# Reciprocals spread through DRAM, value tiles composed on GpSimd, convolution weights transposed first

## The chip, the cores and the metric

One core of one Trainium2 chip. The metric is the device time of one execution, in microseconds (us), less is better. Engine names in the profile: PE is TensorE, PEld its weight loads, DVE is VectorE, ACT is ScalarE, POOL is GpSimd, SP is SyncE.

## The reference

Blockwise causal attention, followed by a gated linear unit whose gate is a causal convolution of five taps. Cut to what matters:

```python
# q, k, v: (8 batches, 8 heads, 576, 64); mask in blocks of 64
scores = where(block_i >= block_j, (q @ k.T) / 8, -1e9)
attn = exp(scores - max) / (sum(...) + 1e-9)
x = (attn @ v)                      # heads side by side: (8, 576, 512)
gate = sigmoid(causal_conv5(x, conv_w))
out = (gate * (x @ w_val)) @ w_out
```

## The kernel before

The kernel works in turns `t`, four per batch, each of a pair of heads. Scores of turn `t`, values of turn `t - 6` and the gated unit of turn `t - 9` are interleaved. Once per batch the softmax denominators are made with matmuls against a one-hot matrix; VectorE takes their reciprocals, which must then reach all 128 partitions. These are the parts that matter here (`vec` keeps VectorE's program order; `load` issues from GpSimd, queue 0; outputs go from SyncE, queue 1):

```python
    def compose_v(b):            # value tiles padded and regrouped
        t = vts[b]
        d = v16p.tile([128, 4, 4, 64], fp16, tag="vd")
        s4 = t[:, :, :].rearrange("p (n t) d -> p n t d", n=4)
        vec.tensor_copy(out=d[0:64, :, :, :], in_=s4[0:64, :, 5:9, :])
        for i in range(4):
            vec.tensor_copy(out=d[64:128, :, i, :], in_=s4[64:128, :, 4, :])
        z = vzs[b % 2]
        vec.tensor_copy(out=z[0:64, :, 0:5, :], in_=s4[0:64, :, 0:5, :])
        vec.tensor_copy(out=z[64:128, :, 5, :], in_=s4[64:128, :, 4, :])
    ...
    def den(b):
        dn = psG.tile([128, 9, 32], fp32, tag="G")       # one of 4 PSUM buffers
        ...                                              # 88 matmuls
        ri = rp.tile([128, 288], fp32, tag="ri")
        vec.reciprocal(out=ri[:, :], in_=dn[:, :, :].rearrange("p j x -> p (j x)"))

    def spread(b):
        ri = ris.pop(b)
        for h in range(2):
            for u in range(2):
                for e in range(2):
                    r0, r1 = 32 * (2 * h + u), 32 * (2 * h + e)
                    move = vec if b == 0 and h == 0 else nc.gpsimd
                    move.tensor_copy(out=rqs[b % 2][r0:r0 + 32, e, :], in_=ri[r1:r1 + 32, :])

    def pv(t):
        ...
        rb = rp.tile([128, 2, 9, 32], fp32, tag="rb")
        vec.stream_shuffle(out=rb..., in_=rqs[b % 2]..., mask=[n] * 32)
        for part, (lo, hi) in enumerate(((0, 5), (5, 9))):
            x = psG.tile([128, nb, 64], fp32, tag="G")
            ...                                          # value matmuls into x
            vec.tensor_tensor(out=xb[...], in0=x[...], in1=rb[...], op=ALU.mult)
    ...
    for t in range(NT + LAG):
        b, r = divmod(t, 4)
        scores(t, 0)
        if t % 2 == 0: load_pair(t // 2 + 3)             # one q and one k load
        if r == 0: load_v(b)
        if t in (2, 3, 6, 7): weights(t // 4, t % 2 * 2)
        if r == 0 and b >= 1: compose_v(b - 1)
        if t <= 4: conv_weights(t - 1)                   # -1: transpose, 0 to 3: diagonals
        ...
        if r == 0 and b >= 1: den(b - 1)
        ...
        pv(t - 6)
        ...
        if r == 1 and b >= 1: spread(b - 1)
        gate(...); val(...); project(...)
```

The softmax here doesn't subtract the row's maximum and nothing guards it: scores larger than these inputs give would overflow.

## Time and profile before

| | before |
|---|---|
| median of the first three runs | 242.03 us (241.86 to 243.42) |
| span of the profiled run | 242.0 us |
| PE busy | 220.4 us, 91% |
| DVE busy | 159.6 us, 66% |
| POOL busy | 65.8 us, 27% |

The head of the page. The rows of digits cut the span into 40 slices of 6 us; a digit is the busy share in tenths (9 is 90% or more), and PEclk is TensorE's granted clock.

```profile
span 242.0 us, 7696 instructions
PE 220.4 (91%) x3352; PEld 146.6 (61%) x3352; DVE 159.6 (66%) x340; ACT 139.1 (57%) x232; POOL 65.8 (27%) x110
PE   0799978799989998999989998999989997999993
PEclk9997788979999999999999999999999999999999
DMA  5999999969707990399108980192002200321205
```

TensorE binds from the ninth slice (about 51 us) on. Before that there is a ramp, in which the DMA engines are full and the clock is granted at half speed part of the time. The table of stretches shows the same: each line is a stretch in us, then busy time and count per engine, the granted clock, the DMA share (over 1 where packets overlap) and GB/s.

```profile
core 0: us, PE busy (x) PEld busy (x) DVE busy (x) ACT busy (x) POOL busy (x), PEclk, DMA share, GB/s
7.00:51.00 44.00, 37.45 (x654) 26.36 (x655) 34.28 (x63) 29.19 (x40) 20.74 (x30) 0.85 1.36 157
71.00:90.00 19.00, 19.00 (x256) 11.89 (x254) 12.05 (x25) 12.75 (x23) 6.29 (x9) 1.00 1.05 150
90.00:97.00 7.00, 6.23 (x156) 4.57 (x154) 6.64 (x15) 3.40 (x7) 1.21 (x3) 1.00 0.01 2
```

From 71 to 90 us TensorE has no gap at all. The stretch from 90 to 97 holds a denominator turn, and there 0.77 us are idle. The list of waits (who waited for whom: us in total, times, longest) says for what:

```profile
PE cv L43 <- DVE ri L56: 5.1, 6, 1.2
```

The timeline of VectorE around one such turn (start us, duration us, engine, line, operation, output and inputs, count) shows why, and the last line is TensorE's:

```profile
65.29 1.07 DVE L56 COPY d<-t 64x1024 f16<-64x1024 f16 x5
66.37 0.72 DVE L56 COPY vz_72<-t 64x1280 f16<-64x1280 f16 x2
67.12 1.96 DVE L56 RECIPROCAL ri<-dn 128x288 f32<-128x288 f32 x1
...
69.13 0.77 PE L43 MATMUL cv<-xb_67,diag 128*128 128x288 f16 x5 [0.77 <-DVE ri L56]
```

The convolution's second half needs the PSUM buffer that the reciprocal reads (PSUM tiles are what this kernel's matmuls write into). Composing (`d`, `vz`) delays the reciprocal a little: the denominator matmuls had ended at 66.8.

The first batch in the ramp, its reciprocals and their first use:

```profile
28.52 1.96 DVE L56 RECIPROCAL ri<-dn 128x288 f32<-128x288 f32 x1 [1.20 <-PE dn L43]
...
36.50 0.80 DVE L56 STREAM_SHUFFLE rb<-rq_70 128x576 f32<-128x576 f32 x1
37.40 0.82 DVE L56 TENSOR_TENSOR xb_67<-x,rb 128x320 f16<-128x320 f32 x2
```

There are 7 us between the end of the reciprocals and their first use.

### The profile page before, as it was taken

How to read it: one execution, taken by the hardware profiler on the slowest of the kernel's cores; microseconds unless marked ns; L12 is line 12 of the kernel's file. 1: busy time of each engine (PE TensorE's matmuls, PEld its weight loads, DVE VectorE, ACT ScalarE, POOL GpSimd, SP SyncE). 2: the span in 40 equal slices, each digit the busy share in tenths (PEclk: the TensorE clock that was granted, in tenths of full speed). 3: DMA queues.
4: the chain of work that ended last, by engine and by line, in shares of the span. 5: the costliest groups of instructions: out<-in, count | busy, mean ns of one | idle time of the engine just before them, and what ended most of it. 6: DMA issues, size and time to landing. Idle time of an engine off the chain costs nothing.

```text
span 242.0 us, 7696 instructions
## 1 busy us (share of the span) xinstructions
PE 220.4 (91%) x3352; PEld 146.6 (61%) x3352; DVE 159.6 (66%) x340; ACT 139.1 (57%) x232; POOL 65.8 (27%) x110
## 2 busy tenths in 40 slices
PE   0799978799989998999989998999989997999993
PEld 0565755566765576556756566556755674676661
DVE  3377798967895489846695489756694368556330
ACT  2549686466837664665827755665737853333442
POOL 8950093390058001820057002410050005000000
PEclk9997788979999999999999999999999999999999
DMA  5999999969707990399108980192002200321205
GB/s 95 177 187 195 186 89 192 141 89 163 50 3 126 208 137 3 33 242 197 47 0 147 210 114 5 45 153 88 36 3 89 87 3 3 143 76 63 113 3 213
DMA packets 52010, 25.13 MB, mean 104 GB/s; under 512 B 38149, under 2 KB 47365, under 8 KB 51978
## 3 DMA queue, kind: packets, MB, share of 16 engines
q0 software_dynamic: 46784, 15.21, 58.5%
q1 hardware_dynamic: 5184, 9.44, 10.6%
q8 instruction: 26, 0.43, 0.7%
q14 instruction: 6, 0.05, 0.1%
q10 hardware_dynamic: 10, 0.01, 0.0%
HBM read 30.42 MB, written 9.44 MB: 165 GB/s over the span
## 4 chain that ended last, share of the span: by engine, by line
PE 76%; DVE 12%; ACT 3%; issue 3%; DMA 3%; POOL 0%; ACTq 0%; DVEq 0%; POOLq 0%
PE cv L43 16%; PE ps L43 15%; PE ot L43 13%; PE vp L43 12%; PE tr L131 10%; PE x L43 9%; DVE ri L56 5%; DVE d L56 2%; DMA t<-in_k_dram 2%; ACT pt L168 2%; DVE gv L56 2%; DVE qkT L56 2%; PE dn L43 2%; ACT pt L194 1%; DVE vz_73 L56 1%
## 5 line engine op out<-in xcount | busy, mean ns | idle before, releaser
L168 ACT ACTIVATE pt<-ps 128x1024 f16<-128x1024 f32 (+1 forms) x96 | 75.6, 825 | 16.2 <-PE ps L43 15.6
L56 DVE COPY qkT<-tr 128x768 f16<-128x768 f16 (+1 forms) x62 | 49.6, 836 | 33.4 <-PE tr L131 32.3
L43 PE MATMUL ps<-qkT 64*64 64x64 f16 (+10 forms) x608 | 45.6, 257 | 3.8 <-ACT pt L194 1.4
L328 ACT ACTIVATE th<-cv 128x288 f32<-128x288 f32 x64 | 26.2, 412 | 32.9 <-PE cv L43 30.9
L356 ACT ACTIVATE ob<-ot 128x512 f32<-128x512 f32 x36 | 21.7, 602 | 33.8 <-PE ot L43 28.7
L56 DVE SCALAR_TENSOR_TENSOR gv<-th,vp 128x288 f16<-128x288 f32 x64 | 26.9, 446 | 18.4 <-PE vp L43 18.0
L43 PEld LDWEIGHTS <-qkT 64*64 64x64 f16 (+1 forms) x608 | 21.3, 105 | 28.1 <-issue 19.8
L43 PEld LDWEIGHTS <-diag 128*128 128x128 f16 x320 | 28.9, 98 | 14.8 <-issue 6.2
L43 PE MATMUL ot<-w_out_sb,gv 128*128 128x512 f16 x144 | 35.8, 380 | 0.0
L131 PE MATMUL tr<-ident_59,t 128*64 128x128 f16 x576 | 28.5, 242 | 6.8 <-DMA t<-in_q_dram 5.5
L259 POOL COPY rq_71<-ri 32x288 f32<-32x288 f32 x32 | 13.4, 420 | 65.1 <-DVE ri L56 63.5
L259 POOL COPY rq_70<-ri 32x288 f32<-32x288 f32 x28 | 11.8, 420 | 65.5 <-DVE ri L56 64.1
L43 PE MATMUL x<-pt,t 128*64 128x256 f16 (+3 forms) x384 | 28.0, 257 | 1.7 <-issue 1.7
L131 PEld LDWEIGHTS <-t 128*64 128x64 f16 x576 | 20.0, 121 | 13.9 <-DMA t<-in_q_dram 5.5
L43 PEld LDWEIGHTS <-w_val_sb 128*128 128x128 f16 x256 | 23.1, 98 | 7.6 <-issue 0.2
L194 ACT ACTIVATE pt<-ps 128x512 f16<-128x512 f32 x32 | 19.1, 598 | 10.5 <-PE ps L43 9.1
L43 PEld LDWEIGHTS <-t 128*64 128x64 f16 x384 | 18.5, 113 | 10.5 <-issue 8.1
L43 PEld LDWEIGHTS <-gv 128*128 128x128 f16 x144 | 12.7, 98 | 13.7 <-issue 2.1
L43 PE MATMUL cv<-xb_67,diag 128*128 128x288 f16 x120 | 17.6, 292 | 1.5 <-DVE ri L56 1.5
L43 PE MATMUL cv<-xb_68,diag 128*128 128x288 f16 x120 | 17.1, 286 | 1.5 <-DVE ri L56 1.5
L56 DVE RECIPROCAL ri<-dn 128x288 f32<-128x288 f32 x8 | 15.7, 1958 | 1.4 <-PE dn L43 1.2
L46 POOL DMA_DIRECT2D t<-in_v_dram x8 | 14.6, 1826 | 5.1 <-PE x L43 4.7
(51 smaller groups left out, 234.7 us busy)
## 6 DMA issues: line engine op xcount, KB each, us to landing
out_dram<-ob SPq DMA_DIRECT2D x36, 256.0 KB, 2.1
t<-in_q_dram POOLq DMA_DIRECT2D x16, 288.0 KB, 7.0
t<-in_k_dram POOLq DMA_DIRECT2D x16, 288.0 KB, 7.9
t<-in_v_dram POOLq DMA_DIRECT2D x8, 576.0 KB, 13.1
w_val_sb<-in_moe_w_val_dram POOLq DMA_DIRECT2D x2, 256.0 KB, 13.6
w_out_sb<-in_moe_w_out_dram POOLq DMA_DIRECT2D x2, 256.0 KB, 6.7
conv_nat<-in_moe_conv_w_dram ACTq DMA_DIRECT2D x1, 10.0 KB
```

Of the source, the lines that this page charges most:

```text
L43: tc.keep_in_program_order(nc.tensor.matmul(**kw))
L46: tc.keep_in_program_order(nc.gpsimd.dma_start(**kw))
L56: return lambda **kw: tc.keep_in_program_order(f(**kw))
L131: tc.keep_in_program_order(nc.tensor.transpose(out=tr[64 * z:64 * z + 64, s, :], in_=q16[hb, w][:, z, c, :], identity=ident16[:, :]))
L168: nc.scalar.activation(out=pt[:, o:o + w], in_=src, func=AF.Exp, bias=0.0, scale=0.125)
L194: nc.scalar.activation(out=pt[:, 2048:2560].rearrange("p (h x) -> p h x", h=2), in_=ps[:, :, 0:256], func=AF.Exp, bias=0.0, scale=0.125)
L259: move.tensor_copy(out=rqs[b % 2][r0:r0 + 32, e, :], in_=ri[r1:r1 + 32, :])
L328: nc.scalar.activation(out=th[:, HF * hf:HF * hf + HF], in_=cv[:, :], func=AF.Tanh, bias=0.0, scale=0.5)
L356: nc.scalar.mul(out=ob[:, :], in_=ot[:, :], mul=0.5)
```

## The change

Its intent is to unload VectorE. The reciprocals are written once to DRAM and read back by four broadcast reads per batch, so that the 32 shuffles and 64 copies of the on-chip way go. Composing of the value tiles moves to GpSimd, one turn earlier. The transpose of the convolution weights moves ahead of the first q and k transposes.

```diff
+    rscr = nc.dram_tensor("r_scratch", [B, 128, 288], fp32, kind="Internal")
@@ compose_v
-        vec.tensor_copy(out=d[0:64, :, :, :], in_=s4[0:64, :, 5:9, :])
-        for i in range(4):
-            vec.tensor_copy(out=d[64:128, :, i, :], in_=s4[64:128, :, 4, :])
+        nc.gpsimd.tensor_copy(out=d[0:64, :, :, :], in_=s4[0:64, :, 5:9, :])
+        nc.gpsimd.tensor_copy(out=d[64:128, :, :, :],
+                              in_=s4[64:128, :, 4:5, :].to_broadcast([64, 4, 4, 64]))
         ... the two copies into z likewise
@@ spread: the copies go
+        nc.sync.dma_start(out=rscr[b], in_=ris.pop(b)[:, :])
+        rb = rp.tile([128, 4, 2, 9, 32], fp32, tag="rb", name="rb")
         for h in range(2):
+            for e in range(2):
+                r0 = 32 * (2 * h + e)
+                nc.sync.dma_start(
+                    out=rb[64 * h:64 * h + 64, :, e, :, :].rearrange("p n j y -> p n (j y)"),
+                    in_=rscr[b, r0:r0 + 4, :].rearrange("(a r) x -> a r x", a=1).to_broadcast(
+                        [64, 4, 288]))
+        rbs[b] = rb
@@ pv: the stream_shuffle goes
-                in1=rb[:, :, lo:hi, :].rearrange("p e j y -> p j e y"),
+                in1=rbs[b][:, n, :, lo:hi, :].rearrange("p e j y -> p j e y"),
@@ setup and loop
+    conv_weights(-1)
     for part in range(3):
         trans(0, part)
-        if r == 0 and 1 <= b <= B:
-            compose_v(b - 1)
-        if t <= 4:
+        if r == 3 and b < B:
+            compose_v(b)
+        if 1 <= t <= 4:
             conv_weights(t - 1)
         if r == 0 and 1 <= b <= B:
             den(b - 1)
+            spread(b - 1)
-        if r == 1 and 1 <= b <= B:
-            spread(b - 1)
```

More of the change, by code (lines that the diff above doesn't have):

```diff
@@ L75 @@
            for i in range(NXB)]
-    rqs = [cpool.tile([128, 2, 288], fp32, tag=f"rq{i}", name=f"rq{i}") for i in range(2)]
     vzs = [cpool.tile([128, 4, 6, 64], fp16, tag=f"vz{i}", name=f"vz{i}") for i in range(2)]
@@ L110, in compose_v @@
         s4 = t[:, :, :].rearrange("p (n t) d -> p n t d", n=4)
-        vec.tensor_copy(out=d[0:64, :, :, :], in_=s4[0:64, :, 5:9, :])
-        for i in range(4):
-            vec.tensor_copy(out=d[64:128, :, i, :], in_=s4[64:128, :, 4, :])
+        nc.gpsimd.tensor_copy(out=d[0:64, :, :, :], in_=s4[0:64, :, 5:9, :])
+        nc.gpsimd.tensor_copy(out=d[64:128, :, :, :],
+                              in_=s4[64:128, :, 4:5, :].to_broadcast([64, 4, 4, 64]))
         z = vzs[b % 2]
-        vec.tensor_copy(out=z[0:64, :, 0:5, :], in_=s4[0:64, :, 0:5, :])
-        vec.tensor_copy(out=z[64:128, :, 5, :], in_=s4[64:128, :, 4, :])
+        nc.gpsimd.tensor_copy(out=z[0:64, :, 0:5, :], in_=s4[0:64, :, 0:5, :])
+        nc.gpsimd.tensor_copy(out=z[64:128, :, 5, :], in_=s4[64:128, :, 4, :])
         vts[b] = (t, d, z)
@@ L248, in den @@
         ris[b] = ri
+    rbs = {}
     def spread(b):
-        ri = ris.pop(b)
+        nc.sync.dma_start(out=rscr[b], in_=ris.pop(b)[:, :])
+        rb = rp.tile([128, 4, 2, 9, 32], fp32, tag="rb", name="rb")
         for h in range(2):
-            for u in range(2):
-                for e in range(2):
-                    r0, r1 = 32 * (2 * h + u), 32 * (2 * h + e)
-                    move = vec if b == 0 and h == 0 else nc.gpsimd
-                    move.tensor_copy(out=rqs[b % 2][r0:r0 + 32, e, :], in_=ri[r1:r1 + 32, :])
+            for e in range(2):
[5 more added lines that the diff above has]
+        rbs[b] = rb
     def pv(t):
@@ L266, in pv @@
         xb = xbs[b % NXB]
-        rb = rp.tile([128, 2, 9, 32], fp32, tag="rb")
-        vec.stream_shuffle(out=rb[:, :, :, :].rearrange("p e j y -> p (e j y)"),
-                                 in_=rqs[b % 2][:, :, :].rearrange("p e x -> p (e x)"),
-                                 mask=[n] * 32)
         for part, (lo, hi) in enumerate(((0, 5), (5, 9))):
```

## The prediction

> **What bounds the kernel now.** The page gives TensorE (PE) 220.4 us busy of 242.0 (91%), VectorE (DVE) 66%, GpSimd (POOL) 27%. By stretches, PE is busy without a gap from 71 to 90, 97 to 117, 124 to 144, 151 to 171 and 203 to 235 us: PE binds from about 51 us on. Its 21.6 us of idle time are about 5.5 at the start, 4 after the last matmul, 5 to 6 in the ramp from 7 to 51 us (DMA row at 9, granted clock down to 0.8), and a gap of 0.77 us in each later denominator turn (list of waits: "PE cv <- DVE ri 5.1 us, 6 times"). So 40 us less DVE work cannot become 40 us less time.
>
> **What the change does.** From DVE it removes 32 shuffles (25.5 us), the composing of value tiles (14 us, 1.8 per batch) and four copies (1.4). From POOL it removes 60 copies of 420 ns (25 us) and adds 32, about 4 us per batch (estimate from those 420 ns for 288 elements). It adds one 147 KB write and four 295 KB broadcast reads per batch on the SyncE queue: 8192 pieces of 1152 B in all. The output's 2048-byte pieces took 88 ns; I estimate 55 to 60 ns for these, 4 us of all 16 engines per batch. It moves 1.9 us of small fp32 matmuls (at 10.4 us) into the wait for the first q load, which ends at 5.4.
>
> **What of it is critical.**
> - Later turns: in the timeline the denominator matmuls end at 66.8 and the reciprocal runs 67.1 to 69.1, only 0.3 us late for DVE's composing. The next convolution group still waits for its PSUM buffer: gap 0.77 becomes about 0.4, a gain of 2 to 2.5 us in all.
> - Weights first: gain 1 to 1.5 us. DVE relief in the ramp: 0.5 to 1.
> - First batch: reciprocal at 28.5 to 30.5 us, first use at 37.4, just when GpSimd's loads fill the DMA engines. The Trainium skill, "DMA: Bandwidth & Descriptors", section "Issuing engines are not separate DMA queues", says transfers from all issuers share the same 16 engines and interleave; this trace agrees: an output tile lands in 2.1 us in quiet, 5.5 to 7.8 beside loads. So write 3 to 5 us, reads 6 to 10: landed at 40 to 45. DVE stalls at the first multiplication; PE runs on until the next turn's value matmuls want that PSUM buffer (about 39). Loss 2 to 7 us, mid 4.5. Second batch: 0 to 2. Later batches have 16 us from denominators to first use and need 10 to 12: no stall.
> - Composing on GpSimd holds later loads about 10 us back in the ramp; they have that slack.
>
> Sum: about -4.5 gain, +5.5 loss: **243.0 us, range 238.5 to 248.5**. Faster by over 2%: 0.06; within 2%: 0.73; slower by over 2%: 0.21.
>
> **What would show it.** DVE near 120 us busy, PE near 220. "PE cv <- DVE ri" still there, about 0.4 us each. A DVE wait of several us at the first multiplication into xb for the reads of rb, at 36 to 44 us, with PE idle behind it; in later batches none. Reads landing in 6 to 10 us in the ramp, 4 to 6 later. Convolution-weight matmuls before 5.5 us. GpSimd copies of 1024 elements about 1.2 us.
>
> **What would make it wrong.** If the reads get only one piece between long runs of load descriptors, they land at 50 or later and the loss passes 10 us. If the loads leave a lull at 30 to 36 us, as before, the stall vanishes and the kernel gains 3 to 4 us. If later reads last over 12 us, every batch stalls.

## The result, and the profile after

The changed kernel took 254.91 us (median of 4 runs, 252.72 to 256.18); before took 242.54 us in the same rounds. The ratio is 1.050, with a 95% interval of 1.042 to 1.058. Ratios here and below are the mean time of one kernel's fast runs over that of the other's of the same rounds, so not quite the ratio of the medians quoted. Executions over 1.5% slower than the fastest of the same kernel are left out of the means.

| | before | after |
|---|---|---|
| median | 242.54 us | 254.91 us |
| span of the profiled run | 242.0 us | 254.3 us |
| PE busy | 220.4 us | 224.2 us |
| DVE busy | 159.6 us | 120.2 us |
| POOL busy | 65.8 us | 71.3 us |

The head of the page after:

```profile
span 254.3 us, 7582 instructions
PE 224.2 (88%) x3352; PEld 148.6 (58%) x3352; DVE 120.2 (47%) x216; ACT 139.2 (55%) x232; POOL 71.3 (28%) x82
PE   3799970298899999999999999999999999799993
PEclk9999995569999999999999999999999999979999
DMA  6999899994991899189935990599129202920305
```

VectorE lost 39 us of work, as intended, and the kernel got 12 us longer. The hole is in PE's seventh and eighth slices ("0", "2"), and the clock falls to half in the same place. The list of waits after, TensorE's and VectorE's:

```profile
PE x L44 <- DVE xb L57: 12.1, 1, 12.1
PE cv L44 <- DVE ri L57: 2.9, 6, 0.5
PE vp L44 <- DVE xb L57: 2.6, 2, 1.6
...
DVE xb L57 <- DMA rb<-r_scratch: 18.5, 2, 13.5
```

A single wait of 12.1 us is as large as the whole loss. The chain of waits shows its parts (start us, duration us, what):

```profile
28.14 1.97 DVE ri L57
...
30.13 6.96 DMA r_scratch<-ri
...
37.10 0.68 SPq L259
...
39.14 9.56 DMA rb<-r_scratch
...
48.82 0.50 DVE xb L57
49.32 0.04 issue
49.36 0.85 PE x L44 x7
```

VectorE reached its first multiplication into `xb` at 35.3 us and stood there 13.5 us, until 48.8. TensorE ran on to 37.3 us and then needed a PSUM buffer that this multiplication frees. In the packet records, the write of 147 KB issued at 30.1 has its first piece at 33.9 and its last at 36.6; the reads issued from 37.1 have theirs from 40.7 to 48.0.

Where the time lies over the kernel is best seen from a mark that both traces have: the first denominator matmul of each batch, in us from the start.

| batch | 0 | 1 | 2 | 3 | 4 | 5 | 6 | 7 | end |
|---|---|---|---|---|---|---|---|---|---|
| before | 26.1 | 42.1 | 65.2 | 91.7 | 119.1 | 145.5 | 173.0 | 197.1 | 242.0 |
| after | 25.2 | 53.3 | 75.9 | 102.1 | 129.2 | 155.4 | 182.6 | 206.4 | 254.3 |
| difference | -0.9 | +11.2 | +10.7 | +10.4 | +10.1 | +9.9 | +9.6 | +9.3 | +12.3 |

The start gains 0.9 us (weights first, though the ramps differ in clock too: the first record of full speed is at 17.5 us before and at 28.4 after). The first batch loses 12.1. Each denominator turn from batch 2 on gains 0.2 to 0.3. The tail loses 3.0: VectorE waits there once more for `rb`, 5.0 us in the last batch, until 222.3 us; TensorE loses 1.6 us to that, and its clock is at half for 3.4 us just after. The denominator turn itself, after:

```profile
77.53 1.96 DVE L57 RECIPROCAL ri<-dn 128x288 f32<-128x288 f32 x1 [1.48 <-PE dn L44]
...
79.54 0.78 PE L44 MATMUL cv<-xb,diag 128*128 128x288 f16 x5 [0.36 <-DVE ri L57]
```

### The profile page after: what moved, and what is told of

It is laid out like the page before. It is cut to its first block, busy times and chain, and to the rows that moved or that the text cites. A ratio compares the mean times of both kernels' runs of the same rounds, so it can differ in the third digit from the quotient of the medians.

```text
span 254.3 us, 7582 instructions
## 1 busy us (share of the span) xinstructions
PE 224.2 (88%) x3352; PEld 148.6 (58%) x3352; DVE 120.2 (47%) x216; ACT 139.2 (55%) x232; POOL 71.3 (28%) x82
## 4 chain that ended last, share of the span: by engine, by line
PE 69%; DMA 17%; DVE 7%; SPq 2%; ACT 2%; issue 1%; POOL 0%; DVEq 0%; ACTq 0%; POOLq 0%
PE cv L44 13%; PE vp L44 12%; PE ps L44 12%; PE ot L44 11%; DMA rb<-r_scratch 9%; PE tr L131 8%; PE x L44 7%; DVE ri L57 6%; PE dn L44 6%; DMA r_scratch<-ri 5%; SPq L259 2%; DMA t<-in_k_dram 2%; DMA out_dram<-ob 1%; ACT pt L168 1%; ACT pt L194 1%
## 5 line engine op out<-in xcount | busy, mean ns | idle before, releaser
L44 PE MATMUL ps<-qkT 64*64 64x64 f16 (+10 forms) x608 | 46.8, 262 | 3.4 <-DVE qkT L57 1.2
L57 DVE TENSOR_TENSOR xb<-x,rb 128x320 f16<-128x320 f32 x64 | 26.9, 447 | 47.9 <-PE x L44 25.2
L44 PE MATMUL cv<-xb,diag 128*128 128x288 f16 x320 | 46.2, 286 | 3.4 <-DVE ri L57 2.9
L44 PE MATMUL vp<-xb,w_val_sb 128*128 128x288 f16 x256 | 37.8, 291 | 2.6 <-DVE xb L57 2.6
L44 PE MATMUL x<-pt,t 128*64 128x256 f16 (+3 forms) x384 | 27.1, 253 | 12.1 <-DVE xb L57 12.1
L44 PE MATMUL ot<-w_out_sb,gv 128*128 128x512 f16 x144 | 36.7, 387 | 0.0
L44 PEld LDWEIGHTS <-w_val_sb 128*128 128x128 f16 x256 | 23.4, 99 | 10.7 <-issue 3.0
L131 PE MATMUL tr<-ident,t 128*64 128x128 f16 x576 | 28.4, 243 | 1.3 <-DMA t<-in_q_dram 0.6
L115 POOL COPY vz<-t 64x1280 f16<-64x1280 f16 x8 | 10.6, 1329 | 56.1 <-PE x L44 56.0
L111 POOL COPY d<-t 64x1024 f16<-64x1024 f16 x8 | 8.2, 1028 | 64.0 <-DMA t<-in_v_dram 64.0
L44 PEld LDWEIGHTS <-gv 128*128 128x128 f16 x144 | 12.9, 99 | 14.1 <-issue 2.7
## 6 DMA issues: line engine op xcount, KB each, us to landing
t<-in_v_dram POOLq DMA_DIRECT2D x8, 576.0 KB, 11.2
```

What stands on the lines that cost most here:

```text
L44: tc.keep_in_program_order(nc.tensor.matmul(**kw))
L57: return lambda **kw: tc.keep_in_program_order(f(**kw))
L111: nc.gpsimd.tensor_copy(out=d[0:64, :, :, :], in_=s4[0:64, :, 5:9, :])
L115: nc.gpsimd.tensor_copy(out=z[0:64, :, 0:5, :], in_=s4[0:64, :, 0:5, :])
L131: tc.keep_in_program_order(nc.tensor.transpose(out=tr[64 * z:64 * z + 64, s, :], in_=q16[hb, w][:, z, c, :], identity=ident16[:, :]))
```

## The experiments

The theory: the loss is the first batch's round trip through DRAM, made long because the loads of queue 0 stand before it on the DMA engines. Rivals: composing on GpSimd pushes the loads back onto the spread (rival 1); composing on GpSimd or weights first cost the time themselves (rival 2); every DRAM spread costs something (rival 3); the round trip is just as slow without loads beside it (rival 4). The edits below are shortened to what matters.

### The DRAM spread alone

```diff
 the kernel before
+        spread(b) through DRAM as in the change, called after den(b)
-        the copies and the stream_shuffle
```

> The kernel before with nothing changed but the way of the reciprocals (DRAM write and four reads, placed after the denominators). Theory (the loss is the first batch's round trip through DRAM, held up behind the loads of queue 0): here nothing holds the loads back any more, so queue 0 is as full as in the changed kernel or fuller; the wait of the first multiplication for rb is 12 us or more, TensorE idles 10 to 16 us once, total 252 to 260 us. Rival 1 (composing on GpSimd, which pushes the loads from 14 to 26 us, is what makes the spread late): stall under 6 us, total under 248. Rival 2 (the loss comes from GpSimd composing itself or from the weights first): total within 2% of before, 240 to 246.

Measured: 255.7 us (254.3 to 261.1; the longest run is slow), ratio 1.049; TensorE's wait for the multiplication 11.2 us, once:

```profile
PE x L44 <- DVE xb L57: 11.2, 1, 11.2
```

This is the whole loss of the change, so rivals 1 and 2 fall: neither of the other two parts is needed for it.

### All but the DRAM spread

```diff
 the changed kernel
-        DRAM write and reads
+        copies into rqs and stream_shuffle, as before
```

> The changed kernel with the reciprocals spread on the chip again (copies and shuffles as before); composing on GpSimd and weights first stay. Theory: no stall for rb; the two other parts together gain about 1 us at the start and 0.3 us per denominator turn, total 238.5 to 241 us, a little faster than before. Rival 2 (composing on GpSimd or weights first cost time): 250 us or more.

Measured: 245.0 us (244.3 to 245.5), ratio 1.006 (0.997 to 1.015). The DRAM loss is gone, but the expected 238.5 to 241 is missed. The second denominators came at 38.9 us, 3.3 us earlier than before; then TensorE idled 6.6 us for VectorE, which waited 7.9 us for GpSimd. GpSimd's timeline there:

```profile
41.91 1.84 POOL L46 DMA_DIRECT2D t<-in_v_dram  x1
51.86 1.03 POOL L111 COPY d<-t 64x1024 f16<-64x1024 f16 x1 [8.11 <-DMA t<-in_v_dram]
52.95 1.04 POOL L112 COPY d<-t 64x1024 f16<-64x1024 f16 x1
54.05 3.68 POOL L259 COPY rq<-ri 32x288 f32<-32x288 f32 x8
```

The copies that spread batch 1's reciprocals (`rq`), ready at 42.4 us, sit in GpSimd's queue behind the composing of batch 2 (`d`), which waits for its values to land. The scheduler had put them in that order. So composing on GpSimd did cost time here, not by its work but by what it puts ahead of something urgent.

### The same, with GpSimd's copies in program order

```diff
 all but the DRAM spread
+    pool = Ordered(nc.gpsimd)      # keeps program order, as vec does
-    nc.gpsimd.tensor_copy(...) in compose_v and spread
+    pool.tensor_copy(...)
```

> As the run with all batches spread on the chip, composing on GpSimd and weights first, which gave 245.0, but with GpSimd's copies kept in program order. That run had gained 3.3 us on before at the second denominators and lost 6.6 us when the copies of batch 1's reciprocals sat on GpSimd behind the composing of batch 2, which waited for its load. Theory: without that wait 3 us at the ramp and 2 us in the denominator turns are kept: 236 to 239 us, faster than before by 1.5 to 2.5%. Rival (composing on GpSimd itself costs what it gains): 241 us or more.

Measured: 236.65 us (234.9 to 238.3), ratio 0.978 (0.972 to 0.983). As expected, and faster than both kernels, though the interval is not wholly below 0.98. Part of the gain may be the clock's: the profiled run is the fastest of the six and its clock records show full speed from 15.3 us on without a break, where the kernel before has 13.7 us at half speed up to 51.6 us. No run separates the two. Its timeline of GpSimd at the same place shows the copies following the loads at once:

```profile
41.80 1.83 POOL L46 DMA_DIRECT2D t<-in_v_dram  x1
43.68 3.67 POOL L56 COPY rq<-ri 32x288 f32<-32x288 f32 x8
...
51.27 2.12 POOL L56 COPY d<-t 64x1024 f16<-64x1024 f16 x2 [2.56 <-DMA t<-in_v_dram]
```

### Only the first batch on the chip

```diff
 the changed kernel
+    spread on the chip for batch 0, through DRAM for 1 to 7
```

> The changed kernel with only the first batch's reciprocals spread on the chip; seven batches still go through DRAM. Theory: the 12 us stall is gone, the wait of the last batch (5 us on VectorE, 1.6 to 3.5 us in all) stays: total 241 to 244.5 us. Rival 3 (every DRAM spread costs about 1.5 us, by contention or by its reads): about 10 of the 12 us stay, total above 251.

Measured: 247.3 us (247.0 to 248.0), ratio 1.017. The first stall is gone and rival 3 with it, in the size it had named, but the total is above the range. The stall moved on: batch 1 now reaches its denominators at 38.6 us, in the middle of the loads, instead of 53.3, and pays for its own round trip. From the chain of waits of this run:

```profile
40.27 1.97 DVE ri L58
...
42.26 5.62 DMA r_scratch<-ri
...
50.15 9.84 DMA rb<-r_scratch
...
60.11 0.50 DVE xb L58
60.65 1.12 PE vp L45 x4
```

TensorE lost 7.3 us to it. In the changed kernel batch 1 was spared: after batch 0's stall the loads had drained, and the packet records show no piece of queue 0 between the issue and the end of batch 1's write and 119 beside its reads, against 1872 and 345 in this run.

### Batches 0, 1 and 7 on the chip

```diff
 the changed kernel
+    spread on the chip for batches 0, 1 and 7, through DRAM for 2 to 6
+    GpSimd's copies in program order
```

> The changed kernel with batches 0, 1 and 7 spread on the chip and 2 to 6 through DRAM; the copies on GpSimd kept in program order, so that those of batch 1 do not queue behind the composing of batch 2, which waits for its values. Theory (only the batches with little time between denominators and first use, or with full DMA engines, pay for DRAM): no stall of TensorE over 1 us for rb, total within 1.5 us of the run with all on the chip in this order, 236 to 240 us. Rival 3 (DRAM spreads in the middle cost too): 2 us or more above that run.

Measured: 237.68 us (237.5 to 237.9), ratio 0.982 (0.975 to 0.988), 1.0 us above the run with all on the chip, which the two intervals do not tell from none. In its list TensorE waits for no multiplication into `xb` longer than 0.2 us, and VectorE for the reads of `rb` once, 2.9 us. So five batches can go through DRAM nearly free of charge; the cost belongs to the two in the ramp and the last.

### Loads held back until the first reads have landed

```diff
 the changed kernel, t == 4
+    nc.gpsimd.tensor_copy(out=held, in_=rbs[0][:, 0, :, 0, 0])   # in order, waits for the reads
+    load_v(1)                    # taken from its old place; all later loads come after it
```

> The changed kernel, but v of batch 1 and all later loads are issued only when the first batch's reads have landed (a small GpSimd copy reads rb before them). Theory (queue 0 holds back queue 1): the write lands within 2 to 3 us of its issue instead of 7.0, the reads begin 1.5 us after theirs instead of 3.6, rb is there at 40 to 42 us instead of 48.7, TensorE idles 3 to 5 us instead of 12.1, total 245 to 248 us. Rival 4 (the round trip is slow in itself, load or no load): write 7 us, rb at 47 or later, total 253 or more.

Measured: 260.8 us (260.4 to 261.8), ratio 1.073. The total is far off; the step under test came near what was expected, if not quite so short. The first batch's chain in this run:

```profile
29.73 3.88 DMA r_scratch<-ri
...
35.64 6.44 DMA rb<-r_scratch
...
42.21 0.50 DVE xb L57
42.71 0.04 issue
42.75 0.37 PE x L44
```

The write took 3.9 us instead of 7.0 (expected 2 to 3), the last read 6.4 instead of 9.6, and TensorE idled 6.0 us instead of 12.1 (expected 3 to 5). In the packet records no piece of queue 0 lies in the stretch of the reads. Most of what was saved lay before a first piece, not in the pieces: the write's first came 0.9 us after its issue instead of 3.8, the reads' first 1.5 instead of 3.6, while the reads' pieces lasted 6.3 us instead of 7.2. So half of the first stall is the loads beside it, and half is the round trip alone; rival 4 falls for the one half and holds for the other. The loads held back then met the second batch's spread: VectorE waited up to 11.9 us for `rb` there, and TensorE 8.7 us for VectorE.

### Reads in pieces of 4608 bytes

```diff
 the changed kernel
-        rb = rp.tile([128, 4, 2, 9, 32], ...)    # four rows of 1152 B per partition and read
+        rb = rp.tile([128, 2, 4, 9, 32], ...)    # one run of 4608 B per partition and read
         ... the patterns of the reads and of pv to match
```

> The changed kernel with the reads in pieces of 4608 B instead of 1152 (256 per batch instead of 1024), the same bytes. If a read piece costs per piece (1152 B took 85 ns, 2048 B of the outputs 88): the reads' pieces last 3 to 4.5 us instead of 6.2 to 7.3, the first stall shrinks from 12.1 to about 9 us and the last one vanishes, total 249 to 252 us. Rival (the rate is set by bytes, 188 GB/s, since all partitions read the same rows): 6 us or more as before, total 253 to 256.

Measured: 251.95 us (249.9 to 254.3; the longest run is slow), ratio 1.038. The total lies in the first range, but the pieces did not get as short as that theory said: the reads last 5.6 to 7.2 us per batch (before this edit 6.2 to 7.2), a piece of 4608 B takes 314 ns where one of 1152 B takes 88, and the first stall is 11.2 us instead of 12.1. So four times the bytes took 3.6 times as long: the bytes set most of the time, not the count of pieces. 1.18 MB in 6.1 us, the mean, are 193 GB/s.

### Weights first alone, composing alone

```diff
 the kernel before
+    conv_weights(-1)           # ahead of the first transposes, and nothing else
```

> The kernel before with the convolution weights transposed first and nothing else. Theory: 1.9 us of TensorE work moves into the wait for the first q load; the first value matmuls come 0.7 to 1 us earlier, and what of it survives to the end is 0 to 1.5 us: total 0.994 to 1.000 of before. Rival: the extra work delays the first transposes and the total is 1 us or more longer.

Measured: 240.6 us (239.3 to 242.8), ratio 0.996 (0.990 to 1.002): a small gain that these rounds do not tell from none.

```diff
 the kernel before
-        vec.tensor_copy(...) in compose_v, at r == 0
+        pool.tensor_copy(...) in compose_v, at r == 3; GpSimd's copies in program order
```

> The kernel before with composing moved to GpSimd alone, GpSimd's copies kept in program order; spread on the chip, weights where they were. Theory: the gap of 0.77 us in the denominator turns becomes 0.5 (2 us in all) and VectorE in the ramp is freed; with weights first alone at 0.996 and both together at 0.978, this part alone is 0.980 to 0.990 of before, 238 to 241 us. Rival (the gain of the two together came from weights first and from calmer clocks): 0.995 to 1.005.

Measured: 238.75 us (237.0 to 239.6), ratio 0.987 (0.982 to 0.991). As expected: composing on GpSimd is worth 1.3%, in the order that keeps the reciprocals' copies ahead. In its profile 3.0 of the 5.1 us gained lie ahead of batch 2's denominators (62.2 us against 65.2), in the ramp, and about 0.3 us in each turn of denominators after that. What of the ramp's part is the calmer clock (no half speed after 30.0 us) is not shown.

### TensorE kept busy in the stall

```diff
 the changed kernel, t == 7, ahead of pv(1)
+    for i in range(45):
+        mm(out=ps[:, 0, :], lhsT=ident16[:, :], rhs=q16[5, 0][:, :, 0:4, :], ...)   # no one reads it
```

> The changed kernel with 45 matmuls of 512 columns without use put ahead of the second head pair's value matmuls, where TensorE idles 12.1 us for rb; they last about 10 us and delay nothing that isn't waiting. If the halved clock of 38.6 to 55.7 us in the changed kernel comes from TensorE idling: no halved stretch after 49 us, the second denominators take 1.6 us instead of 2.7, total 251 to 253 us. If it comes from somewhere else: the halved stretch stays or moves, the useless matmuls then last up to 20 us, total 254 to 262 us. Either way the wait of VectorE for rb stays 12 to 14 us.

Measured: four runs of 251.8 to 257.5 us, two of them slow (by their time; their mean clocks, 0.983 and 0.985, are not below the 0.982 of the fastest); the two fast ones are 251.8 and 252.1. In the changed kernel the clock records have half speed from 38.6 to 55.7 us. Here, after 3.4 us from 22.7, there is none until 50.0, and then 3.4 us, after TensorE had idled 2.8 us once the useless matmuls had run out. That slow stretch fell on the second denominators, which took 2.6 us; the expected 1.6 was missed. That fits the clock following TensorE's idling, but does not show it. With times that spread this far and one profile, what the slower clock cost in the changed kernel is not settled; I put it at 1 to 3 us as an estimate, from its second denominators taking 2.7 us where the same matmuls take 1.6 at full clock, over some 6 us of such work.

## Why the prediction was wrong

It said 243.0 us (238.5 to 248.5) and "within 2%" as the likeliest; measured were 254.9 us and 5.0% slower. The mechanism was right: "DVE stalls at the first multiplication; PE runs on until the next turn's value matmuls want that PSUM buffer". Shown: the wait of 13.5 us at just that instruction, and DRAM spread alone giving the whole loss. The term that was mis-sized is "Loss 2 to 7 us, mid 4.5", which measured 12.1 us. The reads landed 6.2 us after the middle of "40 to 45" and TensorE needed the buffer 1.7 us before "about 39"; together that is 7.9 us, nearly the 7.6 between 4.5 and 12.1. The parts:

- "write 3 to 5 us" measured 7.0. Held clear of later loads it took 3.9.
- "reads 6 to 10: landed at 40 to 45". From the first issue at 37.1 to the landing at 48.7 it was 11.6 us: 3.6 to the first piece and 7.2 from there to the end of the last, then the signal. The four reads must also be issued one after the other, 0.6 to 0.7 us each; the term names neither that nor the wait for a first piece.
- "I estimate 55 to 60 ns for these". The write's pieces of 1152 B took 55 ns, the reads' 88: five batches that shared the DMA engines with next to nothing still needed 6.2 to 6.9 us for the pieces of their reads, not 4. The estimate was scaled down from writes of 2048 B to DRAM and used for reads in which 64 partitions at a time take the same rows. No run reads rows of its own into each partition on this queue, so whether the shared rows are what costs is not shown.
- "first use at 37.4", "about 39" for TensorE: it was 35.3 and 37.3. The gains that the same text had promised (weights first, no shuffle ahead of the multiplication) bring the first use forward, and thus lengthen the wait. The sum had counted them as gain only.

The text's own warning, that the loss would pass 10 us if reads got one piece between long runs of load descriptors, came true in its number, but not through slow reads: queue 0's pieces filled a third of the engines' time beside the reads (0.34), and the reads' pieces lasted 7.2 us against 6.2 to 6.9 in quiet batches. The rest, point by point:

- "Second batch: 0 to 2" came out right, with no wait for `rb`, but by luck: the first stall, longer than foreseen, had let the loads drain. Where that stall was taken away (only the first batch on the chip), TensorE lost 7.3 us to the second batch.
- "Later batches ... no stall" was right for batches 2 to 6 and wrong for the last: 5.0 us of VectorE, 1.6 of TensorE. From the end of its reciprocals (210.0 us) to where VectorE stood waiting (217.2) there were 7.2 us. The turns are shorter once no scores are left, and the 16 us of the earlier turns were carried over to them.
- "Gap 0.77 becomes about 0.4": 2.9 us in six turns, 0.48 each; gained 0.2 to 0.3 us per turn. Right.
- "Weights first: gain 1 to 1.5 us": 0.9 at the first denominators (2.2 in the profile of this part alone, whose clock had its first record of full speed at 16.4 us); 0.4% alone and not told from nothing.
- "Composing on GpSimd holds later loads about 10 us back ... they have that slack": the first held-back load went out at 26.1 us instead of 14.1, and TensorE waits for none of them. Right, and the DRAM spread alone shows that this holding back is not the cause.
- "DVE near 120 us busy, PE near 220": 120.2 and 224.2.
- Not seen at all: the clock at half for 17 us from the stall on. The Trainium skill, "TensorE: Matmul & The Clock Gate", section "HAM oscillation — how this bites in real kernels", warns of idle gaps of TensorE over about 3.4 us, after which it is throttled. This trace has half speed in the long gap, but agrees with that size only in part: it was recorded from 38.6 us, 1.3 us after idling began at 37.3, and again from 223.0 after a gap of 1.6 us. In the kernel before it began at 20.9, 34.6 and 48.2 us, though no gap of TensorE from 7 to 51 us is longer than 1.7 us. What sets the clock is thus not shown here.

That transfers from all issuers share the DMA engines, which the prediction took from the skill, fits: with the loads away, the stall halved. Its page "DMA: Bandwidth & Descriptors", section "Queues, rings and completion order", says that an engine serves its queues in turn, a packet each; here queue 1's first piece came 3.8 us after its issue with queue 0 full, against 0.8 to 0.9 in quiet batches. No run here shows whether the turns or something before them made that wait.

## What to carry to other kernels

Work that leaves an engine off the critical path buys only the gap that it had left on the critical engine (here 0.3 us per batch once the ramp is over), while a round trip through DRAM put in its place is paid for wherever the time from producing to first use is short: check the first, the second and the last iteration by themselves, not the steady state. A stall taken away in one iteration can come back in the next, because the stall had also given the loads time to drain. When work moves to an in-order queue, look at what urgent work it may come to stand before: keeping program order there turned no gain (ratio 1.006) into one of 2.2% (0.978, in other rounds).

## What the Trainium skill lacked or had wrong

- "DMA: Bandwidth & Descriptors" gives no rate for a read in which many partitions take the same DRAM rows. The runs show 1.18 MB in 6.2 to 6.9 us (171 to 190 GB/s) with next to nothing beside it, hardly better with pieces four times as long (6.1 us on average). The outputs' 2048-byte pieces took 88 ns in the kernel before; by an estimate from that, 16 engines at once would write 372 GB/s.
- The same page's section "Issuing engines are not separate DMA queues" calls the issuing time "usually small relative to the DMA itself". Four reads took 2.6 us to issue from SyncE one after the other, against 6 to 7 us of transfer.
- "GPSIMD Engine Reference", section "Engine selection", puts one-input work at roughly line rate and gives a factor, about 2 against VectorE, only for two inputs. Here a one-input copy of 1024 fp16 elements took 1.03 us on GpSimd and 0.41 us on VectorE, 2.5 times as long, so that row alone misleads for such copies.
- "TensorE: Matmul & The Clock Gate" says in its Part 1 that the default state is throttled; the runs agree (12 transposes took 0.85 us at 12 to 15 us in the kernel before, against 0.53 later), but the profile's row of granted clock shows 9 for the first slices all the same. The first record of full clock came between 15 and 30 us in different runs. The skill does not say what such a row shows ahead of its first record.
- The same page's gap of about 3.4 us, cited above, is not where half speed began in these runs: gaps of 1.6 us (before 223.0 us, after) and 1.7 us (before 48.2 us, kernel before) came ahead of it too, while gaps of 1.7 us at 214 us (only the first batch on the chip) and 2.0 us at 66 us (TensorE kept busy) did not lead to it.
